# Attention and MLP in one kernel: another opening, DMA transposes for the later chunks, and the MLP's features loaded before attention

## The chip, the cores and the metric

The kernel runs on one core of a Trainium2 chip. The metric is the device time of one execution in microseconds (us); the span in a profile is a little shorter than the time of the execution it comes from. Engines: PE (TensorE, matrix products; PEld are its weight loads), DVE (VectorE), ACT (ScalarE), POOL (GpSimd) and SP (SyncE, which here only issues transfers). A "warm" matmul computes nothing that is used; it keeps PE busy.

## The reference

Shapes: x is 2048 x 640, 32 heads of 20, MLP width 1536.

```python
x  = A_x
xn = layernorm(x)                                   # no weights
qkv = (xn @ wqkv).reshape(B, S, 3, H, Dh)
p   = softmax(q @ k.T * Dh**-0.5)                   # per head
a   = (p @ v).reshape(B, S, D) @ wo
y   = layernorm(xn)
m   = gelu(y @ w1 + b1) @ w2 + b2                   # tanh form of gelu
out = x + a + m
```

## The kernel before, in words

Products run on f16 pairs: an f32 value is kept as a high half and a low half, and a product is three passes (`PASS`: high-high, high-low, low-high), accumulated in PSUM.

**Head** (lines 155 to 509, instruction order written out by hand). The 2048 rows are four chunks of 512 (`c`), each of four 128-row tiles (`j`). For a chunk, `norm_a` takes mean and variance on DVE and a power on POOL, `norm_b` refines it and normalises the four tiles in place, `norm_c` finishes the second norm's factor and writes it to `rscr`. `transp` turns the tiles on PE into PSUM tiles `pt`, two of the five 128-column slices (`k`) at a time; `transp_out` splits them into the halves `xnt` (ACT writes the high half, DVE the low one) and the last call writes the whole chunk to `xscr` for the MLP.

`qk(c, tt)` is one product of 30 matmuls for two of the ten 128-row blocks of Q and K, `qk_out` scales and splits it (`qkhl`), squares it (`sq`) and writes it to `qkscr`. `lengths` multiplies pending squares by `heads`, which gives squared lengths of every head's vectors; `shifts` makes one row `brow` of softmax shifts out of their maxima. `vproj(c, j)` is the V product of one tile, `vproj_out` puts it into `vfull`. The next chunk's norms and transposes are placed among the five `tt` steps of the current one. `some(n)` advances the preparation of w1 and w2 (squares for a scale, then splits) by n steps. `sums` and `scale_of` find a weight's power-of-two scale (the latter with a PE product `mxp`), `split_qkv` splits a weight of wqkv.

All of `transp`, `qk` and `vproj` share three PSUM tiles (`psS`, two banks each); `psO` and `psM` have one tile each.

**Attention** (lines 512 on). For each of 16 head pairs and two halves of the queries, groups of four 128-key blocks: `scores` on PE, exp on ACT, `rest` (a low half of some blocks) on DVE, and `pv` one group later. After the second block of each group a generator `fill` (the MLP, then the output projection) issues PE work: `credit` grows by `rate` = 1.235 a group, each step's cost is taken from it, and a stretch ends when credit or `CHUNK` is used up or an accumulation is complete. The MLP's first yield, 2.0, is a debt that the credit starts with. `load_chunk(mc)` loads 256 columns of features (`xm`) and their factors (`r2f`). `finish` divides by the softmax sums after a number of filler steps (`W1`, `W2` for the last) and writes `oscr`; `projection` loads a piece of it (`ot`) and the sum so far (`acc`), multiplies by wo (`z`) and writes the output.

Of the kernel before, what the change touches and what calls it, by code (L numbers as in the profile page):

```python
# [7 lines left out]
F32 = mybir.dt.float32  # L8
# [34 lines left out]
def mha_mlp_kernel(tc, x, wqkv, wo, w1, b1, w2, b2, out):  # L43
# [4 lines left out]
    with (  # L48
# [3 lines left out]
        tc.tile_pool(name="st", bufs=2) as stp,  # L52
        tc.tile_pool(name="psS", bufs=3, space=PSUM) as psS,
# [99 lines left out]


        with tc.tile_pool(name="pa", bufs=2) as pa, tc.tile_pool(name="pa1", bufs=1) as pa1, tc.manual_schedule():
# [46 lines left out]
            brow = pa1.tile([H, S], F16, name="brow")  # L202
# [33 lines left out]
            def norm_b(c):  # L236
# [5 lines left out]
                for j in range(4):  # L242
                    nc.vector.tensor_scalar(xts[c][j], xts[c][j], mv[:, j, 0:1], r[:, j : j + 1],
                                            ALU.subtract, ALU.mult)
                nc.vector.tensor_mul(ve, ve, mv[:, :, 1])
# [28 lines left out]

            PASS = ((0, 0), (0, 1), (1, 0))

            def qk(c, tt):
                ps = psS.tile([P, 2, 512], F32, tag="s", name="qkp")
                order = [(i, k) for i in range(2) for k in range(KD)]
                if c + tt == 0:  # L280

                    order = [(i, k) for k in range(KD) for i in range(2)]
                for i, k in order:
                    q, mm = divmod(2 * tt + i, KD)
                    for n, (a, b) in enumerate(PASS):
                        nc.tensor.matmul(ps[:, i, :], wv[:, k, q, a, mm * P : (mm + 1) * P],  # L286
                                         xnts[c][:, k, b, :], start=(k + n == 0), stop=(k == KD - 1 and n == 2))
                return ps
# [4 lines left out]
            def qk_out(c, tt, ps):  # L293
# [3 lines left out]
                sq = pa.tile([P, 2, 512], BF16, tag="sq", name="sq", bufs=2)  # L297
                for i0, i1 in parts:
# [3 lines left out]
                                                   ALU.mult, ALU.subtract)  # L302
                if c == 0:
# [3 lines left out]
                for s in range(2):  # L307
                    nc.sync.dma_start(
                        qkscr[s, 2 * tt * P : (2 * tt + 2) * P, c * 512 : (c + 1) * 512]
                        .rearrange("(i p) t -> p i t", p=P), hl[:, s])  # L310
                pend.extend((c, 2 * tt + i, sq[:, i]) for i in range(2))

            def lengths():

                for c, m, sq in pend:
# [10 lines left out]
                pend.clear()  # L326

            def shifts():
# [12 lines left out]
                nc.sync.dma_start(bscr[:H, :], brow)  # L341
# [37 lines left out]
            def split_qkv(n):  # L379
                q = "qkv".index(n)  # L380
                for k in range(KD):
                    nc.scalar.activation(wv[:, k, q, 0], stage[n][:, k], AF.Copy, scale=scales[n])
                    nc.vector.scalar_tensor_tensor(wv[:, k, q, 1], stage[n][:, k], scales[n], wv[:, k, q, 0],
                                                   ALU.mult, ALU.subtract)
# [61 lines left out]
            nc.gpsimd.memset(brow, KROW)  # L446
# [636 lines left out]
```

## Time and profile before

| | |
|---|---|
| median of 3 runs | 1384.71 us (1384.6 to 1388.05) |
| the profiled execution, its own time | 1385.2 us |
| its span | 1383.5 us |
| mean granted PE clock | 0.997 |
| busy PE / DVE / ACT | 1350.8 / 1061.7 / 1126.2 us |
| first Q/K product of the first chunk starts | 21.16 us |
| first scores start | 232.47 us |

A line of the timeline gives start, duration, engine, line of the code, operation, output and inputs, shapes and count; in brackets stands the idle time of the engine before it and what ended it. SPq is SP's queue, where the duration is that of the issuing, waits included. In a table of stages, PEclk is the granted clock as a share of full speed and DMA the busy share of the 16 DMA engines.

### The profile page before, as it was taken

The page shows a single profiled execution, that of the slowest core. Times are in us where ns is not written, and L with a number is a line of the kernel's source. Part 1 is how long each engine was busy: PE and PEld are TensorE (multiplying, and loading weights), DVE is VectorE, ACT ScalarE, POOL GpSimd, SP SyncE. Part 2 cuts the span into 40 slices and gives each one's busy share as a digit, 9 for nine tenths or more (in the row PEclk, how much of TensorE's full clock was granted, in tenths as well). Part 3 has the DMA queues.
Part 4 walks back from the last instruction along what each step waited for, and adds up shares of the span by engine and source line. Part 5 has one row for each costly group of instructions (what it writes and reads, how often), then busy time and mean ns, then how long its engine had stood idle before and what let it go on. Part 6 is the DMA issues. An engine that isn't in the chain of part 4 may idle for free.

```text
span 1383.5 us, 29113 instructions
## 1 busy us (share of the span) xinstructions
PE 1350.8 (98%) x11711; PEld 600.9 (43%) x11711; DVE 1061.7 (77%) x1425; ACT 1126.2 (81%) x1282; POOL 32.9 (2%) x75
## 2 busy tenths in 40 slices
PE   9999999999999999999999999999999999999998
PEld 6555555443333343433343333343334334333375
DVE  6648743899778977889887789877988897888642
ACT  5644323999999999999999999999999999999700
POOL 2000000000000000000000000000000000000000
PEclk9999999999999999999999999999999999999999
DMA  9853413012124231213221123212124322341375
GB/s 265 243 175 109 108 52 110 16 32 64 41 55 111 67 88 34 69 52 102 71 77 33 47 75 103 76 47 58 44 64 113 98 56 70 85 153 59 98 235 179
DMA packets 92320, 125.68 MB, mean 91 GB/s; under 512 B 16905, under 2 KB 58569, under 8 KB 92178
## 3 DMA queue, kind: packets, MB, share of 16 engines
q1 hardware_dynamic: 89218, 117.14, 28.3%
q0 software_dynamic: 2304, 5.24, 2.3%
q8 instruction: 94, 1.54, 0.5%
q10 hardware_dynamic: 656, 1.36, 0.3%
q14 instruction: 48, 0.39, 0.1%
HBM read 80.84 MB, written 42.86 MB: 89 GB/s over the span
## 4 chain that ended last, share of the span: by engine, by line
PE 59%; DVE 11%; ACT 5%; DMA 3%; issue 2%; SPq 1%; DVEq 0%; ACTq 0%
PE o L615 23%; PE s L584 14%; PE py L819 9%; PE pu L787 8%; DVE low L598 5%; PE z L896 5%; ACT p L586 4%; DMA oscr<-oa 1%; DVE u L740 1%; DMA oa<-opart 1%; DVE u L741 1%; DVE w L744 1%; DVE w L745 1%; DVE hT L752 1%; DVE u L750 1%
## 5 line engine op out<-in xcount | busy, mean ns | idle before, releaser
L586 ACT ACTIVATE p<-s 128x1024 f32<-128x1024 f32 x1024 | 973.6, 1042 | 52.4 <-PE s L584 46.2
L598 DVE TENSOR_TENSOR low<-p 128x1024 f16<-128x1024 f32 x512 | 608.8, 1219 | 165.0 <-ACT p L586 164.9
L615 PE MATMUL o<-p,vfull 128*32 128x512 bf16 (+1 forms) x4096 | 433.7, 494 | 0.0
L584 PE MATMUL s<-qs,ks 61*128 61x512 f16 x2048 | 317.7, 382 | 8.7 <-ACT p L586 7.2
L584 PEld LDWEIGHTS <-ks 61*128 61x128 f16 x2048 | 63.9, 94 | 296.4 <-issue 294.2
L787 PE MATMUL pu<-xm,w1t 128*128 128x256 f16 x1440 | 179.2, 274 | 4.1 <-DVE u L740 3.6
L819 PE MATMUL py<-w2t,hT 128*128 128x320 f16 x1152 | 178.6, 301 | 1.7 <-DVE xb L757 1.7
L787 PEld LDWEIGHTS <-w1t 128*128 128x128 f16 x1440 | 130.9, 98 | 71.2 <-issue 57.6
L819 PEld LDWEIGHTS <-hT 128*128 128x128 f16 x1152 | 102.5, 98 | 89.5 <-issue 55.2
L286 PE MATMUL qkp<-xnt,wv 128*128 128x512 f16 x600 | 132.3, 380 | 0.0
L615 PEld LDWEIGHTS <-vfull 128*32 128x32 f16 x3072 | 61.5, 95 | 146.2 <-issue 115.4
L615 PE MATMUL o<-low,vfull 128*32 128x512 f16 x1024 | 107.3, 379 | 6.6 <-DVE low L598 6.4
L300 ACT ACTIVATE qkhl<-qkp,qks 128x1024 f16<-128x1024 f32 (+1 forms) x24 | 23.3, 971 | 84.1 <-PE qkp L286 66.2
L286 PEld LDWEIGHTS <-wv 128*128 128x128 f16 x600 | 58.2, 98 | 67.8
L615 PEld LDWEIGHTS o<-p,vfull 128*32 128x32 f32 x2048 | 63.1, 109 | 50.6 <-issue 0.5
L349 PE MATMUL vp<-wv,xnt 128*128 128x320 f16 x480 | 66.6, 300 | 0.0
L896 PE MATMUL z<-w1t,ot 128*128 128x320 f16 x480 | 65.8, 300 | 0.0
L896 PEld LDWEIGHTS <-ot 128*128 128x128 f16 x480 | 46.7, 98 | 19.8 <-issue 1.7
L349 PEld LDWEIGHTS <-xnt 128*128 128x128 f16 x480 | 46.5, 98 | 18.2
L301 DVE SCALAR_TENSOR_TENSOR qkhl<-qkp,qks,qkhl 128x1024 f16<-128x1024 f32 (+1 forms) x24 | 26.5, 1104 | 34.3 <-ACT qkhl L300 34.3
L857 DVE SCALAR_TENSOR_TENSOR acc<-z,sc,acc 128x320 f32<-128x320 f32 x32 | 17.6, 550 | 45.1 <-PE z L896 42.9
L636 ACT ACTIVATE ev<-o 128x512 f32<-128x512 f32 x64 | 39.4, 615 | 3.3 <-PE o L615 3.3
(168 smaller groups left out, 685.7 us busy)
## 6 DMA issues: line engine op xcount, KB each, us to landing
qkscr<-qkhl SPq DMA_DIRECT2D x40, 256.0 KB
opart<-ev SPq DMA_DIRECT2D x124, 80.0 KB
ks<-qkscr SPq DMA_DIRECT2D x120, 80.0 KB
qs<-qkscr SPq DMA_DIRECT2D x192, 40.0 KB
oa<-opart SPq DMA_DIRECT2D x32, 240.0 KB
xt<-in_A_x_dram SPq DMA_DIRECT2D x16, 320.0 KB
xscr<-xnt SPq DMA_DIRECT2D x4, 1280.0 KB
xm<-xscr SPq DMA_DIRECT2D x8, 640.0 KB
```

Of the source, the lines that this page charges most:

```text
L286: nc.tensor.matmul(ps[:, i, :], wv[:, k, q, a, mm * P : (mm + 1) * P], xnts[c][:, k, b, :], start=(k + n == 0), stop=(k == KD - 1 and n == 2))
L300: nc.scalar.activation(hl[:, 0, i0:i1], ps[:, i0:i1], AF.Copy, scale=a)
L301: nc.vector.scalar_tensor_tensor(hl[:, 1, i0:i1], ps[:, i0:i1], a, hl[:, 0, i0:i1], ALU.mult, ALU.subtract)
L349: nc.tensor.matmul(ps[:, hf, :320], xnts[c][:, k, a, j * P : (j + 1) * P], wv[:, k, 2, b, hf * 320 : (hf + 1) * 320], start=(n == 0), stop ...
L584: nc.tensor.matmul(ps[:, a, :], ks[64 * a : 64 * a + 61, kb * P : (kb + 1) * P], qs[64 * a : 64 * a + 61, cc * 512 : (cc + 1) * 512], star ...
L586: nc.scalar.activation(pt, ps, AF.Exp, scale=QS)
L598: nc.vector.tensor_sub(low, pt, upper(pt))
L615: nc.tensor.matmul(pv.o[32 * q : 32 * q + 32, :], src[:, v0 - PAD * (1 - q % 2) :][:, :32], t, start=q not in pv.begun, stop=last, skip_gr ...
L636: nc.scalar.activation(evs[g, hf][:, cc], pv.o, AF.Copy)
L787: nc.tensor.matmul(ps[:, i], w1v[:, k, (f + i) // 4, a, fo_ : fo_ + P], xnt[:, k, b, :], start=(n == 0), stop=(n == 3 * KD - 1))
L819: nc.tensor.matmul(ps[:, :320], hTs[mc][:, f, a, j * P : (j + 1) * P], w2v[:, f, b, hf * 320 : (hf + 1) * 320], start=(n == 0), stop=(n == ...
L896: nc.tensor.matmul(ps[:, :320], ot[:, k, a, j * P : (j + 1) * P], wov[:, k, b, h * 320 : (h + 1) * 320], start=(n == 0), stop=(n == 3 * KD ...
```

## The change

- x's rows are loaded into two tiles of the pool `m2` (two 128-row tiles in each), which later hold the MLP's features, instead of five tiles of their own. `load_features` loads features; the first two calls stand in the head, at the third step of the last chunk.
- Opening: `brow` is a quarter as long and filled earlier; the first chunk is turned tile by tile into five separate banks, and then slice after slice is split together with the first 256 columns of that slice of wq. Columns 256 to 511 follow after the first product, the last 128 in the second step. Ten instead of twelve calls' worth of warm-up products. `norm_b2`, the second half of `norm_b`, is deferred for the first chunk, and `scale_of("k")` stands in the middle of the second product.
- The second chunk is turned on PE as before, but between the V products of the first. The third and fourth are turned by `turn`: ACT and DVE make the halves of a tile untransposed (`row`), and a transposing transfer on SP's queue writes them into `xnt`.
- `lengths` is called twice a chunk: for four blocks at the fourth step, and for six after the second V product (after the first in the last chunk). Squares of odd steps use another pool's tiles.
- Attention: the credit starts at 0 instead of -2, and in the first group, which has no `pv` yet, the filler gets a second turn.

```diff
+        tc.tile_pool(name="m2", bufs=2) as m2,
...
+        def load_features(mc):
+            xnt = m2.tile([P, KD, 2, MC], F16, tag="xnt", name="xm")
+            nc.sync.dma_start(xnt, xscr[:, :, :, mc * MC : (mc + 1) * MC])
+            return xnt
...
             def load_x(c):
                 xts[c] = []
                 for j in range(4):
-                    xt = pa.tile([P, D], F32, tag="xt", name="xt", bufs=5)
+                    if j % 2 == 0:
+                        pair = m2.tile([P, KD, 2, MC], F16, tag="xnt", name="xt").bitcast(F32)
+                        pair = pair.rearrange("p k s t -> p (k s t)")
+                    xt = pair[:, j % 2 * D : (j % 2 + 1) * D]
                     nc.sync.dma_start(xt, x2[c * 512 + j * P : c * 512 + (j + 1) * P, :])
...
-            brow = pa1.tile([H, S], F16, name="brow")
+            brow = pa1.tile([H, S // 4], F16, name="brow")
+            nc.gpsimd.memset(brow, KROW)
...
+                if c > 0:
+                    norm_b2(c)
+            def norm_b2(c):
+                mv, ve, r, r2 = rs[c]
                 nc.vector.tensor_mul(ve, ve, mv[:, :, 1])
                 nc.vector.tensor_scalar(ve, ve, EPS, None, ALU.add)
                 nc.gpsimd.tensor_tensor(r2, ve, nhalf, ALU.pow)
...
+            def turn(c, j):
+                if j == 0:
+                    xnts[c] = pa.tile([P, KD, 2, 512], F16, tag="xnt", name=f"xnt{c}")
+                xv = xts[c][j].rearrange("p (k n) -> p k n", k=KD)
+                row = pa.tile([P, KD, 2, P], F16, tag="row", name="row", bufs=3)
+                nc.scalar.activation(row[:, :, 0, :], xv, AF.Copy)
+                nc.vector.tensor_sub(row[:, :, 1, :], xv, row[:, :, 0, :])
+                nc.sync.dma_start(xnts[c].rearrange("p k s t -> p (k s) t")[:, :, j * P : (j + 1) * P],
+                                  row.rearrange("p k s n -> p (k s n)"), transpose=True)
+                if j == 3:
+                    nc.sync.dma_start(xscr[:, :, :, c * 512 : (c + 1) * 512], xnts[c])
+                    del xts[c]
...
-            def qk(c, tt):
+            def qk(c, tt, mid=None):
...
-                if c + tt == 0:
+                if c == 0 and tt < 2:
                     order = [(i, k) for k in range(KD) for i in range(2)]
...
+                    if mid and (i, k) == (1, 2):
+                        mid()
...
-            def lengths():
-                for c, m, sq in pend:
+            def lengths(n):
+                for c, m, sq in pend[:n]:
...
-                nc.sync.dma_start(bscr[:H, :], brow)
+                nc.sync.dma_start(bscr[:H, :].rearrange("h (r t) -> h r t", r=4), brow[:, None, :].to_broadcast([H, 4, S // 4]))
...
-            pts = []
-            transp(0, 0, pts)
-            scale_of("q")
-            transp(0, 2, pts)
-            transp(0, 4, pts)
-            warm(12)
-            for t in pts:
-                transp_out(*t)
-            split_qkv("q")
+            xnts[0] = pa.tile([P, KD, 2, 512], F16, tag="xnt", name="xnt0")
+            pts = [psS.tile([P, 2, 512], F32, tag="s", name="pt") for _ in range(2)]
+            pt = [pts[0][:, 0], pts[0][:, 1], pts[1][:, 0], pts[1][:, 1]]
+            for j in range(4):
+                if j == 3:
+                    scale_of("q")
+                    pt.append(psM.tile([P, 512], F32, tag="m", name="pt4"))
+                for k in range(KD - 1):
+                    nc.tensor.transpose(pt[k][:, j * P : (j + 1) * P], xts[0][j][:, k * P : (k + 1) * P], ident)
+            for j in range(4):
+                nc.tensor.transpose(pt[4][:, j * P : (j + 1) * P], xts[0][j][:, 4 * P :], ident)
+            warm(10)
+            for k in range(KD):
+                nc.scalar.activation(xnts[0][:, k, 0, :], pt[k], AF.Copy)
+                nc.vector.tensor_sub(xnts[0][:, k, 1, :], pt[k], xnts[0][:, k, 0, :])
+                split_qkv("q", [k], 0, 2 * P)
...
                 for tt in range(5):
-                    ps = qk(c, tt)
-                    lengths()
+                    if c == 0 and tt == 1:
+                        norm_b2(0)
+                        norm_c(0)
+                        ps = qk(0, 1, lambda: scale_of("k"))
+                        hl = qk_out(0, 0, first)
+                        split_qkv("q", c0=4 * P)
+                        split_qkv("k")
+                    else:
+                        ps = qk(c, tt)
+                    if tt == 3:
+                        lengths(4)
                     if c == 0:
                         if tt == 0:
+                            split_qkv("q", c0=2 * P, c1=4 * P)
                             sums("k", [stage["k"][:, 0:3], stage["k"][:, 3:]])
-                            norm_c(0)
-                            scale_of("k")
+                            first = ps
+                            continue
                         elif tt == 1:
-                            split_qkv("k")
-                            norm_a(1)
+                            qk_sq(0, 0, hl)
...
                     else:
-                        if nxt and tt < 3:
-                            (norm_a, norm_b, norm_c)[tt](nxt)
+                        step = tt - (c == 1)
+                        if nxt and 0 <= step < 3:
+                            (norm_a, norm_b, norm_c)[step](nxt)
                             some(1)
                         else:
                             some(2)
                     qk_out(c, tt, ps)
-                    if nxt and tt >= 2:
-                        pts = []
-                        transp(nxt, 2 * (tt - 2), pts)
-                        transp_out(*pts[0])
-                if c + 2 < 4:
-                    load_x(c + 2)
+                    if nxt and c > 0 and tt >= 2:
+                        for j in ((0,), (1, 2), (3,))[tt - 2]:
+                            turn(nxt, j)
+                    if c == 3 and tt == 2:
+                        early = [load_features(mc) for mc in range(2)]
+                if c == 1:
+                    load_x(3)
...
                 for j in range(4):
                     ps = vproj(c, j)
-                    lengths()
+                    if c == 0:
+                        if j == 0:
+                            norm_c(1)
+                        if j < 3:
+                            pts = []
+                            transp(1, 2 * j, pts)
+                            transp_out(*pts[0])
+                    if j == (0 if c == 3 else 1):
+                        lengths(10)
...
                     vproj_out(c, j, ps)
+                if c == 0:
+                    load_x(2)
...
             def mlp():
                 load_chunk(0)
                 load_chunk(1)
-                yield 2.0
+                yield 0.0
...
                             rest(units[0])
                             credit += rate
-                            spent, over[0] = 0.0, False
...
+                            other()
                         else:
                             for u in units[1:]:
                                 rest(u)
                             if prev:
                                 pv(prev)
+                            else:
+                                credit += rate
+                                other()
```

`other()` holds the loop that spends the credit, word for word as it stood. Not shown above: in the first chunk the second chunk's norms and v's scale and split come one step later.

More of the change, by code (lines that the diff above doesn't have):

```diff
@@ L770, in load_chunk @@
                 t0 = mc * MC
-                xnt = m2.tile([P, KD, 2, MC], F16, tag="xnt", name="xm")
-                r2f = m2.tile([P, MC], F32, tag="r2f", name="r2f")
-                nc.sync.dma_start(xnt, xscr[:, :, :, t0 : t0 + MC])
+                xnt = early.pop(0) if early else load_features(mc)
+                r2f = m1.tile([P, MC], F32, tag="r2f", name="r2f", bufs=2)
                 nc.sync.dma_start(r2f, rscr[None, t0 : t0 + MC].to_broadcast([P, MC]))
```

63 lines of the change are left out of this document (37 added, 26 removed).

## The prediction

> **What bounds the kernel now.** I read the page's busy shares and the chain that ended last first, then the timeline stage by stage, with the granted clock beside it.
>
> ```profile
> PE 1350.8 (98%) x11711; PEld 600.9 (43%) x11711; DVE 1061.7 (77%) x1425; ACT 1126.2 (81%) x1282; POOL 32.9 (2%) x75
> PE 59%; DVE 11%; ACT 5%; DMA 3%; issue 2%; SPq 1%; DVEq 0%; ACTq 0%
> 21.16 6.64 PE L286 MATMUL qkp<-xnt,wv 128*128 128x512 f16 x30
> 75.74 13.11 PE L286 MATMUL qkp<-xnt,wv 128*128 128x512 f16 x60
> 88.78 0.30 PE L321 MATMUL norms<-sq,heads 128*32 128x128 bf16 x8
> 89.01 6.65 PE L286 MATMUL qkp<-xnt,wv 128*128 128x512 f16 x30
> 220.14 12.40 PE L349 MATMUL vp<-wv,xnt 128*128 128x320 f16 x90
> 232.47 0.61 PE L584 MATMUL s<-qs,ks 61*128 61x512 f16 x4
> ```
>
> TensorE (PE) is the bound nearly everywhere: 98% busy, and the chain runs through it. So a change is worth what it takes off PE's own queue, or out of the few places where PE waits. The head (opening and projections) ends at 232.47, where the first scores start; attention with the MLP as filler follows, and then a tail of output projections.
>
> Prices on PE from these rows: one Q/K product of 30 matmuls is (88.78-75.74)/2 = 6.52 us; one V product is (232.47-220.14)/3 = 4.11 us; eight length matmuls take 89.01-88.78 = 0.23 us. The projection of a 512-row chunk is thus at least 5x6.52 + 4x4.11 = 49.0 us.
>
> **The opening.** Here PE waits and then runs at half clock.
>
> ```profile
> 1.07 11.38 PE L209 MATMUL warm<-ones 128*128 128x128 f32 x80 [1.07 <-POOL ones L174]
> 10.38 1.79 POOL L446 MEMSET brow<- 32x2048 f16 x1
> 10.85 1.36 DVE L217 TENSOR_SCALAR at<-at 128x4 f32<-128x4 f32 x1
> 24.24 0.17 DVE L217 TENSOR_SCALAR bt<-bt 128x4 f32<-128x4 f32 x1
> 12.83 2.18 DVE L243 TENSOR_SCALAR xt<-xt,mv,r 128x640 f32<-128x640 f32 x4
> 15.49 2.41 PE L262 MATMUL pt<-ident,xt 128*128 128x128 f32 x12
> 17.69 3.63 PE L209 MATMUL warm<-ones 128*128 128x128 f32 x24
> 8.00:10.00 2.00, 2.00 (x20) 1.00 1.02 402
> 16.00:17.00 1.00, 1.00 (x7) 0.50 0.11 29
> 50.75 1.09 PE L262 MATMUL pt<-ident,xt 128*128 128x128 f32 x8
> 51.68 6.64 PE L286 MATMUL qkp<-xnt,wv 128*128 128x512 f16 x30
> ```
>
> The two windows rows give PE's busy time with its instructions, the granted clock, the DMA share and GB/s. One tiny DVE step, L217, takes 1.36 us in the opening and 0.17 in the same code at 24.24; it ends at 12.21, just as the POOL memset of `brow` ends (12.17). The change issues that memset before the statistics and makes it a quarter as long, so L217 falls back to 0.17 and the four normalised rows of x come at 12.2, 12.7, 13.3 and 13.8 instead of from 13.4 to 15.0. The warm-up matmuls end at 12.45, so PE meets the first row at once: its gap there goes, and I take the clock to stay full. At full clock a transpose costs (51.68-50.75)/8 = 0.116 us, against 0.2 in the twelve at 15.49.
>
> Transposing row by row, PE does 20 transposes and the scale's matmul from 12.45 to about 15.1, the last slice's four among them. Then come 20 warm-up matmuls (ten calls instead of twelve) at 2.00/20 = 0.1 us: 17.1. Is the first slice there?
>
> ```profile
> 16.61 0.15 DVE L374 TENSOR_SCALAR s_q<-hi_q 128x1 f32<-128x1 f32 x1
> 48.17 3.69 ACT L382 ACTIVATE wv<-w1t,s_v 128x640 f16<-128x640 f32 x5
> 51.69 4.07 DVE L383 SCALAR_TENSOR_TENSOR wv<-w1t,s_v,wv 128x640 f16<-128x640 f32 x5
> 62.44 0.58 ACT L269 ACTIVATE xnt<-pt 128x512 f16<-128x512 f32 x1
> 63.05 0.69 DVE L270 TENSOR_TENSOR xnt<-pt,xnt 128x512 f16<-128x512 f32 x1 [0.29 <-ACT xnt L269]
> ```
>
> Before, s_q is there at 16.76, 1.75 us after the last normalised row; it now comes near 15.5. One slice is then 0.58 + some 0.4 us on ACT (256 of 640 columns of 0.74) and 0.69 + some 0.45 us on DVE, so slice 0 is complete near 16.6 and each further one 1.1 us later; PE takes six matmuls, 1.3 us, for a slice. The first product starts at 17.1 instead of 21.16: **4.0 us gained**. If the clock still halves, transposes at 0.2 and warm-ups at 3.63/24 = 0.15 put it at 19.9: 1.3. Nothing slower has a cause, so the bounds are 1 and 4.1.
>
> **The first chunk's stage.** It now lasts 75.74-21.16 = 54.6 us.
>
> ```profile
> 42.15 1.91 PE L262 MATMUL pt<-ident,xt 128*128 128x128 f32 x8 [0.39 <-DVE xt L243]
> 62.92 1.26 ACT L415 ACTIVATE junk<-w2t 128x1280 bf16<-128x1280 f32 x1
> 65.57 0.69 ACT L359 ACTIVATE vfull<-vp 128x640 f16<-128x640 f32 x1
> ```
>
> The eight transposes at 42.15 wait for norm_b(1) on DVE and hold PE 1.9 us, 1.0 more than the 0.93 at 50.75. In the new order all of chunk 1's transposes stand behind V products. PE's own work is 49.0 + 40 length matmuls 1.15 + 20 transposes 2.3 + three scale matmuls, priced like eight length matmuls, 0.7 = 53.2 us. But V products and transposes now alternate over three PSUM tiles, and between two of them ACT has up to 1.1 us of transp_out, two squares of 1.26 with their reads, some 2.7, and 0.7 of vproj_out, and DVE 0.8 behind it: a V tile is free some 5.3 us after the transposes, while PE comes back for one after 4.11 us and the lengths, 4.8. That is half a microsecond and more lost in each of two or three places. Also scale_of("k"), moved into the middle of the second product, makes DVE wait in order with qk_out(0, 0) and the splits of q's last columns and of k queued behind it, for which PE's third product then waits. I take 3 us of such waits (bounds 0 and 6): 56.2 us, **1.7 us lost**. norm_b2, norm_c and the deferred squares only change place on DVE and ACT inside this; rscr waits later on SP, and no transfer behind it is due.
>
> **The second and third chunks' stages.**
>
> ```profile
> 116.92 0.30 PE L321 MATMUL norms<-sq,heads 128*32 128x128 bf16 x8 [0.49 <-DVE sq L306]
> L125 ACT ACTIVATE wtmp<-w2t,s 128x640 f32<-128x640 f32 x12 | 9.8, 823 | 4.3 <-DVE w2t L127 4.2
> L127 DVE TENSOR_TENSOR w2t<-wtmp,w2t 128x640 f16<-128x640 f32 x12 | 9.9, 826 | 0.4
> 93.50:94.00 0.50, 0.50 (x4) 0.21 (x3) 0.00 (x0) 0.00 (x0) 0.00 (x0) 1.00 0.51 4
> rscr<-r SPq DMA_DIRECT2D x4, 2.0 KB
> 1255.47 1.66 DMA rb<-linv
> ```
>
> Twenty transposes, 2.3 us, leave PE in each; the 0.49 us wait for a square at 116.92 goes too, as the lengths come one V product later. So **2.8 and 2.3 us gained**. The lengths' matmuls stay as many, so calling them twice a chunk is worth nothing I can price. turn costs ACT and DVE 4x0.82 us a chunk each, about what transp_out cost; PE covers it.
>
> In their place stand four transposing transfers a chunk, which the trace does not show. One moves 128 x 1280 f16, 320 KB. Small pieces have a row: one rscr write is 512 pieces of 4 bytes (2.0 KB), and the window holding most of one (busy of PE, PEld, DVE, ACT and POOL, then clock, DMA share and GB/s) shows 0.51 x 0.5 us x 16 engines = 4.1 us, 8 ns a piece. In 32-byte pieces (10240) a turn is then 5.1 us; in 256-byte rows (1280) 0.64; by single elements (163840) 82. I take about 5, nearest to the middle. The cover: turn(2, 0) can go near 96.5 and chunk 2 starts near 124, so up to 27.5/4 = 6.9 us a turn costs nothing. The xscr write waits on SP for the last turn, with only the next load of x behind it. There can be no gain below zero, the PE side being counted already.
>
> The Trainium skill, "VectorE: DVE Perf Modes", "The three transpose paths", speaks against this: 1309 ns for one 128x128 block by the DMA crossbar, 390 ns on TensorE. Ten blocks singly would be an estimated 13.1 us a turn, and the sum would end near +40 us instead of -10. "DMA: Bandwidth & Descriptors", "Latency and other measured facts", gives 261 GB/s for such transfers, an estimated 1.3 us a turn, which leaves the sum as it is. No run here shows either.
>
> **The start of attention and the tail.**
>
> ```profile
> 239.00:240.00 1.00, 1.00 (x16) 0.50 1.14 329
> 241.55 0.61 PE L584 MATMUL s<-qs,ks 61*128 61x512 f16 x4
> 242.09 1.48 PE L787 MATMUL pu<-xm,w1t 128*128 128x256 f16 x12
> 291.16 1.65 PE o L615 x16
> 1339.27 0.96 SPq L851 DMA_DIRECT2D ot<-oscr  x2
> SPq L851 <- DMA oscr<-oa: 2.3, 1, 2.3
> 1324.37 45.75 PE z L896 x336
> ```
>
> From 232.47 to 241.55 PE does eight score pairs, six MLP matmuls and one group of P.V: 9.1 us, first in gaps behind exp, then at half clock (the windows row, columns as before). With the features loaded early and the credit starting at zero, some 30 MLP matmuls fill the gaps; eight pairs at 0.61/2, 30 matmuls at 1.48/12 and the P.V's 1.65 make 7.8: **1.3 us gained**, and 3.2 us of filler is done earlier. That comes off the tail as eight steps of three z matmuls at 45.75/336 = 0.136, 3.3 us. But the last ot load chain is paced by steps and by DMA: SP waited 2.3 us for oscr and issued at 1339.27, and the fifth piece's z starts, counted 144 matmuls after 1324.37, at 1344.0. With 24 matmuls fewer ahead PE is there at 1340.7, while ot lands (0.96 of issue and 1.7 or more, by the rb transfer) at 1342 or later. So 1.9 of the 3.3 go into a new wait: **1.4 us gained** (bounds 0 and 3.3).
>
> **Sum.** 4.0 - 1.7 + 2.8 + 2.3 + 1.3 + 1.4 = 10.1 us. The profiled execution took 1385.2 us around its span of 1383.5 and would become 1375.1; the median of the runs, 1384.71, is 0.5 below it and becomes 1374.6.
>
> **Rivals.** *Smaller gain:* the clock halves in the opening after all (2.7 less) and the first chunk's waits reach 6 us (3 less): 1380.3. For it, ACT is the fullest engine there; against it, PE's idle gap at 12.45 has a visible cause that goes.
>
> *Slower, by the transfers:* each turn's ten 128x128 blocks go one behind another, each at least the shortest landing here (rb<-linv, 1.66 us): 16.6 us a turn, four 66 us from 96.5, so chunk 2 starts at 163 instead of 124. 39 us twice, less 10.1: 1452. It decides against the change from (27.5+5.05)/4 = 8.1 us a turn. Against it, the bytes and the 8 ns pieces; for it, nothing here but an unseen kind of transfer. By the Trainium skill's 1309 ns a block (the section above) it would be an estimated 1424.
>
> *The filler's early start does nothing:* the tail's chain eats all of it and the start stays at exp's pace: 7.4 us gained, 1377.3. This lies inside my range.
>
> **How the numbers follow.** Forecast with its near variants 0.65; smaller gain 0.13; two of these losses together with stalls elsewhere, within 0.3% (4.2 us, about what a measurement of this kernel can tell from none) 0.08; slower by the transfers 0.14. So faster 0.78, same 0.08, slower 0.14. The low end takes no waits in the first stage and none in the tail (3 + 1.9 more): 1369.5; the high end takes the smaller gain, with a tail and a start worth a little less: 1383. What is left out is the slower case and a few hundredths beside it.
>
> **What would show it.** In the profile after: L217 at 0.17 in the opening; granted clock 1.0 from 12 to 20 and the first qkp matmul near 17; the first scores near 225.1; no pt matmuls after chunk 1's; no PE wait for a transfer at chunks 2 and 3; clock 1.0 through the start of attention; a short PE wait for ot in the tail. I am wrong if the first qkp matmul of chunk 2 waits for a DMA, if the opening's clock still falls to 0.5, or if the first chunk's stage grows by more than 5 us.

## The result, and the profile after

| | kernel before | changed kernel |
|---|---|---|
| time, median (lowest to highest) of 22 runs each | 1385.67 us (1383.9 to 1388.05) | 1382.66 us (1376.62 to 1385.66) |
| profiled execution, time and span | 1385.2 / 1383.5 us | 1382.63 / 1380.9 us |
| first Q/K product starts | 21.16 | 17.07 |
| stage of the first, second, third, fourth chunk | 54.6, 53.6, 52.7, 50.4 | 60.4, 50.0, 49.7, 49.8 |
| first scores, and the scores behind the first P.V | 232.47, 241.55 | 226.94, 234.36 |
| loop's end (`ev` of the last unit) | 1309.68 | 1302.12 |
| last step on VectorE (`acc`) | 1376.79 | 1374.03 |

The change is faster, by 0.25%: the ratio of the times is 0.9975 [0.9966, 0.9984]. The forecast was 10.1 us; 3.0 came. At the loop's end the changed kernel is 7.6 us ahead; at the last step it is 2.8 ahead.

The page of the changed kernel, its busy line and the engines' shares of the chain that ended last:

```profile
PE 1343.7 (97%) x11667; PEld 595.6 (43%) x11667; DVE 1061.3 (77%) x1439; ACT 1128.8 (82%) x1296; POOL 31.2 (2%) x75
PE 75%; DVE 12%; DMA 5%; ACT 5%; issue 2%; SPq 1%; POOL 0%; ACTq 0%; DVEq 0%
```

TensorE is busy 7 us less, and DMA has grown from 3% of the chain to 5%. The timeline of the changed kernel by TensorE, VectorE and GpSimd, up to the first scores (start, duration, instructions; in brackets the idle time before and what ended it):

```profile
7.23 0.51 POOL L213 MEMSET brow<- 32x512 f16 x1
10.69 0.17 DVE L228 TENSOR_SCALAR at<-at 128x4 f32<-128x4 f32 x1
12.25 1.61 PE L496 MATMUL pt<-ident,xt 128*128 128x128 f32 x12 [0.38 <-DVE xt L254]
17.07 10.52 PE L316 MATMUL qkp<-xnt,wv 128*128 128x512 f16 x48
57.15 1.92 PE L278 MATMUL pt<-ident,xt 128*128 128x128 f32 x8 [2.66 <-DVE xt L254]
60.12 7.05 PE L389 MATMUL vp<-wv,xnt 128*128 128x320 f16 x30 [1.06 <-DVE qkhl L332]
68.43 4.25 PE L389 MATMUL vp<-wv,xnt 128*128 128x320 f16 x30
77.47 26.06 PE L316 MATMUL qkp<-xnt,wv 128*128 128x512 f16 x120
127.50 26.06 PE L316 MATMUL qkp<-xnt,wv 128*128 128x512 f16 x120
226.94 0.61 PE L655 MATMUL s<-qs,ks 61*128 61x512 f16 x4
```

The opening is as forecast (17.07 against 17.1). The second and third chunks start without a wait for a transfer. The first chunk's stage has a 2.66 us gap at 54.5, a second of 1.06, and a V product that takes 7.05 us where the next takes 4.25. In the windows of those products (length, busy time of PE, PEld, DVE, ACT and POOL, then granted clock, DMA share, GB/s) the clock is down:

```profile
59.00:60.00 1.00, 0.07 (x1) 0.00 (x0) 1.00 (x2) 0.90 (x1) 0.93 (x1) 0.54 1.02 387
60.00:65.00 5.00, 4.88 (x19) 2.81 (x19) 2.59 (x7) 3.33 (x6) 0.00 (x0) 0.50 1.01 419
65.00:67.00 2.00, 2.00 (x13) 1.29 (x12) 0.00 (x0) 0.00 (x0) 0.00 (x0) 0.78 0.98 347
```

What comes before that gap, on ScalarE and VectorE:

```profile
52.86 1.11 ACT L331 ACTIVATE qkhl<-qkp,qks 128x1024 f16<-128x1024 f32 x1 [4.06 <-DMA qkscr<-qkhl]
54.01 1.28 DVE L332 SCALAR_TENSOR_TENSOR qkhl<-qkp,qks,qkhl 128x1024 f16<-128x1024 f32 x1 [3.99 <-ACT qkhl L331]
56.39 2.18 DVE L254 TENSOR_SCALAR xt<-xt,mv,r 128x640 f32<-128x640 f32 x4
58.78 1.28 DVE L332 SCALAR_TENSOR_TENSOR qkhl<-qkp,qks,qkhl 128x1024 f16<-128x1024 f32 x1
```

ScalarE waits 4.06 us for one of the two `qkhl` buffers, whose write to `qkscr` stands behind the load of w2 (issued at 35.41). VectorE waits with it in qk_out(0, 3), and behind that in VectorE's order stands norm_b(1), whose rows the transposes need.

The tail: the z and rb rows by TensorE, then the piece loads on SP, lt on ScalarE's queue and lt's first use on VectorE, all of the changed kernel:

```profile
1301.98 12.40 PE L966 MATMUL z<-w1t,ot 128*128 128x320 f16 x90
1316.81 2.97 PE L787 MATMUL rb<-lt,sel 64*80 64x64 f32 x32 [2.43 <-DVE lt L778]
1319.71 17.17 PE L966 MATMUL z<-w1t,ot 128*128 128x320 f16 x117
1339.32 0.72 PE L966 MATMUL z<-w1t,ot 128*128 128x320 f16 x2 [2.43 <-DMA ot<-oscr]
1306.88 1.19 SPq L921 DMA_DIRECT2D ot<-oscr  x2
1308.78 0.37 SPq L922 DMA_DIRECT2D acc<-accscr  x1
1308.80 1.15 ACTq L746 DMA_DIRECT2D lt<-lpart  x2
1315.39 0.22 DVE L773 TENSOR_TENSOR lt<-lt 64x64 f32<-64x64 f32 x1 [2.87 <-DMA lt<-lpart]
1317.00:1322.00 5.00, 5.00 (x41) 3.93 (x40) 0.03 (x1) 0.00 (x0) 0.00 (x0) 0.66 0.76 215
```

Where the kernel before ran from the loop's end through rb and z without a stop (rb at 1321.87, 2.50 us), TensorE now stops twice, for lt and for ot, 2.43 us each and 0.32 more for ot's second half; behind the first stop the clock is 0.66. The z matmuls cost 0.147 us each in the 117 behind rb, against 0.136.

### The profile page after: what moved, and what is told of

Read it like the earlier page. It is cut to its first block, busy times and chain, and to the rows that moved or that the text cites. A ratio compares the mean times of both kernels' runs of the same rounds, so it can differ in the third digit from the quotient of the medians.

```text
span 1380.9 us, 29065 instructions
## 1 busy us (share of the span) xinstructions
PE 1343.7 (97%) x11667; PEld 595.6 (43%) x11667; DVE 1061.3 (77%) x1439; ACT 1128.8 (82%) x1296; POOL 31.2 (2%) x75
## 4 chain that ended last, share of the span: by engine, by line
PE 75%; DVE 12%; DMA 5%; ACT 5%; issue 2%; SPq 1%; POOL 0%; ACTq 0%; DVEq 0%
PE o L686 24%; PE s L655 15%; PE py L889 10%; PE pu L857 9%; PE qkp L316 8%; PE vp L389 4%; DVE low L669 4%; ACT p L657 4%; PE z L966 4%; DMA oa<-opart 1%; DMA oscr<-oa 1%; DMA qkscr<-qkhl 1%; DVE u L811 1%; DVE u L812 1%; DVE w L815 1%
## 5 line engine op out<-in xcount | busy, mean ns | idle before, releaser
L686 PEld LDWEIGHTS <-vfull 128*32 128x32 f16 x3072 | 61.5, 95 | 146.2 <-issue 115.3
L966 PE MATMUL z<-w1t,ot 128*128 128x320 f16 x480 | 69.1, 306 | 2.8 <-DMA ot<-oscr 2.8
L389 PE MATMUL vp<-wv,xnt 128*128 128x320 f16 x480 | 69.7, 307 | 1.2 <-DVE qkhl L332 1.1
```

The lines of the kernel that those rows point to most:

```text
L389: nc.tensor.matmul(ps[:, hf, :320], xnts[c][:, k, a, j * P : (j + 1) * P], wv[:, k, 2, b, hf * 320 : (hf + 1) * 320], start=(n == 0), stop ...
L686: nc.tensor.matmul(pv.o[32 * q : 32 * q + 32, :], src[:, v0 - PAD * (1 - q % 2) :][:, :32], t, start=q not in pv.begun, stop=last, skip_gr ...
L966: nc.tensor.matmul(ps[:, :320], ot[:, k, a, j * P : (j + 1) * P], wov[:, k, b, h * 320 : (h + 1) * 320], start=(n == 0), stop=(n == 3 * KD ...
```

## Experiments

My theory had two parts: in the first chunk VectorE's order and then the clock, and in the tail a finish chain that no longer finds enough work beside it. The rivals: the PSUM and ScalarE waits that the prediction named; a cost of the transfers elsewhere; chance.

**e1_norm_early: VectorE's order in the first chunk.**

```
 (tt == 3)  split_qkv("v")
+           norm_b(1)
 (tt == 4)  nc.sync.dma_start(w1t, ...)
-           norm_b(1)
```

> The changed kernel with one edit: norm_b(1) stands right behind the splits of v's columns at tt == 3, ahead of qk_out(0, 3), instead of behind it. My theory: the first chunk's stage lost its time because qk_out(0, 3) sat on VectorE waiting for a transfer (qkhl's buffer, behind the load of w2) with norm_b(1) in the queue behind it, so the transposes of chunk 1 came late and TensorE idled until its clock fell. Then the normalise steps now end near 53.6 instead of 58.6, the transposes start near 55, vproj(0, 1) runs at clock 1.0 in 4.2 us instead of 7.05, the stage lasts some 55 us instead of 60.4, and the time falls by 5 to 6 us, to about 1377. The rival, the prediction's own reason (PSUM tiles and ScalarE's squares between V products): the order on VectorE matters little, the stage stays within 1 us of 60.4, and the time too.

Measured: 1377.22 us, ratio to before 0.9943 [0.9929, 0.9957]. The first stage lasts 71.80-16.87 = 54.9 us. ScalarE, VectorE and TensorE of this kernel:

```profile
52.69 1.11 ACT L331 ACTIVATE qkhl<-qkp,qks 128x1024 f16<-128x1024 f32 x1 [4.10 <-DMA qkscr<-qkhl]
50.92 2.18 DVE L254 TENSOR_SCALAR xt<-xt,mv,r 128x640 f32<-128x640 f32 x4
55.27 1.06 PE L278 MATMUL pt<-ident,xt 128*128 128x128 f32 x8 [0.92 <-DVE qkhl L332]
57.27 4.24 PE L389 MATMUL vp<-wv,xnt 128*128 128x320 f16 x30 [0.94 <-DVE qkhl L332]
```

ScalarE's wait is still there (4.10 us), but norm_b(1) is no longer behind it, and the clock stays up. So ScalarE's wait costs time only through the order on VectorE, and the rival falls. The length of the stage in one profile would not show it: e13 below, with norm_b(1) late, had 54.7 us, but there ScalarE waited only 1.15 us.

**e5_warm_gap: the clock by itself.**

```
+  if j == 0: warm(12, psM, "m")
   transp(1, 2 * j, pts)
+  if j == 0: warm(5, psM, "m")
```

> The changed kernel with warm-up matmuls put into TensorE's two gaps of the first chunk: twelve calls (24 instructions, 2.4 us) ahead of chunk 1's first transposes and five (1.0 us) behind them; nothing else moves. My theory: vproj(0, 1) takes 7.05 us because the idle 2.7 us and 1.1 us before it lower the clock to 0.5. With the gaps filled the clock stays 1.0 there, vproj(0, 1) takes 4.2 to 4.5 us, and the time falls by about 2.8 us, to about 1380; the wait for the normalised rows itself stays. The rival: those 30 matmuls are slow for another reason (PSUM or SBUF being read and written beside them), and neither their time nor the whole changes, or it grows by up to 1 us by the warm-ups.

Measured: 1378.93 us, 0.9956 [0.9942, 0.997]; the stage lasts 57.2 us.

```profile
59.72 4.24 PE L389 MATMUL vp<-wv,xnt 128*128 128x320 f16 x30
60.00:65.00 5.00, 5.00 (x56) 3.81 (x57) 2.26 (x4) 3.06 (x6) 0.00 (x0) 1.00 1.04 420
```

With the gaps filled the clock is 1.0 and the product takes 4.24 us: of the changed kernel's 60.4 us, 2.8 were slow matmuls and not waiting.

**e6_w2_act: the load in front of the writes.** `nc.sync.dma_start(w2t, ...)` became `nc.scalar.dma_start(w2t, ...)`.

> The changed kernel with the load of w2 (3.84 MB) issued from ScalarE's queue instead of SyncE's, at the same place in the program; nothing else moves. My theory: ScalarE waits 4.06 us for a qkhl buffer because the writes of qkhl stand behind that load in one queue. In a queue of their own they need not: ScalarE's wait falls under 1.5 us, norm_b(1) runs 2.5 us or more earlier, the wait for the normalised rows (2.66 us) falls under 1 us, and the time falls by 3 to 5 us. The rival: the engines of the transfers are full with w2's bytes whatever queue they come from, so the wait stays within 1 us of 4.06 and the time within 1 us.

Measured: 1377.38 us, 0.9936 [0.9919, 0.9952]; the stage lasts 54.2 us. ScalarE's qk_out(0, 3) no longer waits (2.25 us are left at qk_out(0, 4)) and the transposes start at 55.25 with no wait for the rows. So the place in the queue behind w2 mattered, not the bytes alone; the times say so more than the stage of one profile, their interval lying clear of the changed kernel's 0.9966 to 0.9984.

**e3_pe_turns: chunks 2 and 3 turned by TensorE again.** `turn(nxt, j)` became `transp(nxt, 2 * (tt - 2), pts); transp_out(*pts[0])`.

> The changed kernel with chunks 2 and 3 turned by TensorE behind qk_out (transp and transp_out) instead of by transfers: that part of the change undone. My theory: the transfers are hidden wholly, so undoing them costs TensorE's 2.3 us for the 20 transposes in each of two stages, and up to a microsecond of wait for PSUM each, as in the kernel before: 5 to 7 us more, about 1389. The rival: the transfers cost something elsewhere (VectorE and ScalarE for the rows, the queue to xscr), so that undoing them gives some of it back: 3 us more or less.

Measured: 1385.80 us, 0.9999 [0.9983, 1.0016], some 3.3 us more than the changed kernel; the two stages last 52.35 and 51.90 us instead of 50.03 and 49.68. That is the 20 transposes, 2.3 and 2.2 us, and nothing else: the expected extra waits for PSUM are missing, and the time expected, 1389, was too high. The transfers are hidden wholly.

**e2_rate and e4_start_old: the tail's share.** e2: `rate = 1.235` became 1.221. e4: `yield 0.0` is 2.0 again, and the first group's second `other()` is out.

> The changed kernel with one constant: rate 1.221 instead of 1.235, so that over the 256 groups 3.6 us less of filler is done inside the attention loop and some 27 z matmuls go back to the tail. My theory: the tail is now set by the last finish chain (lengths, reciprocal, rb, oscr, ot), which counts from the loop's end, and work done earlier only leaves TensorE with less to do beside it. Then the loop ends 3.6 us earlier, the waits before rb and before the fifth piece's z shrink from 2.4 and 2.7 us to under 1 each, the clock stays 1.0, and the time falls by 4 to 8 us, to about 1376. The rival: the loop isn't bound by TensorE alone, or the chain is late by its transfers whatever stands beside it: the tail grows by what the loop gives, and the time stays within 1.5 us.

> The changed kernel with the filler's start undone: the first yield is 2.0 again, and the first group has no second turn of the filler. My theory: at the changed kernel's rate the tail eats what the early start brings, and more: 3.2 us of filler go back to the tail. The start of attention grows by 1.3 to 1.7 us and the waits before rb and before ot shrink by 3 us and more with the clock drops behind them, so the time falls by 2 to 5 us, to about 1379. The rival, the prediction's step: the early start is a gain by itself, and undoing it costs 1.4 to 3 us.

Measured: e2 1372.42 us, 0.9904 [0.989, 0.9918]; e4 1376.74 us, 0.9936 [0.9923, 0.995]. Both waits go (ot keeps 0.8 and 0.4 us), the clock stays 1.0, and the gain is larger than I expected in both. Between the profiles of the changed kernel and e2 the loop is 5.2 us shorter, and the tail is 3.8 us shorter although 27 z matmuls (3.7 us) moved into it. TensorE of e2:

```profile
1295.00 0.99 PE L966 MATMUL z<-w1t,ot 128*128 128x320 f16 x6
1309.89 2.50 PE L787 MATMUL rb<-lt,sel 64*80 64x64 f32 x32
1333.12 25.98 PE L966 MATMUL z<-w1t,ot 128*128 128x320 f16 x190 [0.79 <-DMA ot<-oscr]
```

So undoing one part of the change, the filler's early start, makes the changed kernel faster by some 5.5 us. I had expected the start of attention to grow by 1.3 to 1.7 us in e4; it did not. TensorE of e4, from the first scores to those behind the first P.V:

```profile
226.09 0.61 PE L655 MATMUL s<-qs,ks 61*128 61x512 f16 x4
230.02 0.83 PE L857 MATMUL pu<-xm,w1t 128*128 128x256 f16 x6
233.49 0.60 PE L655 MATMUL s<-qs,ks 61*128 61x512 f16 x4
```

That is 7.40 us with 6 MLP matmuls; the changed kernel takes 7.42 with 30, the kernel before 9.08 with 6. The early filler runs in the gaps behind exp and neither shortens nor lengthens the start. The 1.7 us over the kernel before come without it: TensorE no longer waits 0.54 us for the features, and its clock stays 1.0 (0.50 in the kernel before). All that the early filler brings is work taken off the tail, and at this rate the tail is worse for it: 71.9 us with 447 z matmuls against e4's 67.7 with 474.

**e8_before_rate: the control.** Rate 1.221 in the kernel before.

> The kernel before with rate 1.221 instead of 1.235: a control for e2_rate. My theory: the kernel before has no wait in its tail, so the smaller rate has nothing to save there: 3.6 us of filler move from the loop to the tail, and the time stays within 2 us of before. The rival: 1.221 is better by itself (fewer stalls inside the loop), and the kernel before gains most of the 8 to 10 us that the changed one gained.

Measured: 1399.25 us, 1.0099 [1.0084, 1.0115]: slower by 13.7 us, which neither theory said. This kernel had more work left for the tail than any kernel so far, and yet:

```profile
1312.52 1.64 SPq L851 DMA_DIRECT2D ot<-oscr  x2
1324.42 4.49 PE L716 MATMUL rb<-lt,sel 64*80 64x64 f32 x32 [4.79 <-DVE lt L707]
ACT junk L541 <- DMA w1t<-in_A_wo_dram: 7.0, 1, 7.0
```

The last row is from the waits (total, times, longest): ScalarE, and with it exp, also stood 7.0 us for the load of wo, which is now issued at 1249.4, 0.1 us behind the first piece's ot and acc, instead of at 1232.3. "Too little work beside the chain" can't be the reason for a wait before rb here. The new theory: phase. The load of the next piece (ot and acc, 1280 KB) falls between the loop's end and lt, and lt comes late beside it.

**e9_both_121 and e12_rate_up: amount against phase.** e9: as e7 below, rate 1.21. e12: the changed kernel, rate 1.2525.

> As e7_both, but rate 1.21 instead of 1.221: another 2.8 us of filler go from the loop to the tail. My theory, sharpened by e8_before_rate: what hurts is where the load of the next piece (ot and acc, 1280 KB) falls. If it is issued between the loop's end and the transfer of lt, lt comes late and TensorE waits at rb; e2, e4 and e7 have that load some 2 us ahead of the loop's end. With 1.21 the first piece's z matmuls start only at the loop's end and the next load falls 2 to 4 us behind it: the wait before rb is back (2 to 5 us, with a clock drop behind it), and the time is 1371 to 1378, slower than e7. The rival: only the amount of work left beside the finish chain counts, so more of it is no worse: 1365 to 1368, no wait at rb.

> The changed kernel with rate 1.2525: 4.5 us more filler in the loop, so that the tail meets the pieces at the same phase as e2_rate (some 6 z of a piece done at the loop's end), but with a whole piece less to do. My theory of two separate causes: the wait before rb (a matter of phase) is under 0.7 us, and the wait for ot (a matter of the amount left beside the chain) grows from 2.8 us to 5 to 9 us. The time is then within 4 us of the changed kernel's. The rival, that both waits come from too little work: both grow, rb's above 2.4 us.

Measured: e9 1383.64 us, 0.9989 [0.9979, 0.9998]; e12 1384.42 us, 0.9994 [0.9983, 1.0006]. TensorE's waits in the tail, e9's row first, then e12's:

```profile
PE rb L787 <- DVE lt L778: 4.1, 1, 4.1
PE z L966 <- DMA ot<-oscr: 6.1, 2, 5.8
```

With more work left the wait before rb is back; with a whole piece less than e2, but the right phase, it is gone, and ot's wait has grown. Two causes, as expected. e9 is slower still than I expected, since ScalarE's wait for wo (6.6 us) is back too. The tails of all these kernels beside each other, with the issue of the next piece's ot counted from `ev`:

| kernel | ot issued, from the loop's end | lt waited for | TensorE waits at rb | TensorE waits for ot |
|---|---|---|---|---|
| before | -2.8 us | 0 | 0 | 0 |
| changed | +4.8 | 2.87 | 2.43 | 2.75 |
| e2, e4, e7 | -3.0, -2.8, -3.0 | 0 | 0 | 0.8, 0.4, 0.6 |
| e12 | -3.7 | 0 | 0 | 6.1 |
| e8, e9 | +3.8, +3.5 | 4.8, 4.5 | 4.8, 4.1 | 0 |

**e11_hold and e13_behind_lt: the load itself.** e11 held the load in the program until lt was asked for; e13 put it on lt's own queue:

```
-  nc.sync.dma_start(ot[...], ...)   # and acc
+  go = (nc.scalar if ended[0] and c < NMC // 2 else nc.sync).dma_start
+  go(ot[...], ...)
```

> The changed kernel (rate 1.235) with the load of a next piece held back, once the loop has ended, until the last finish has asked for lt: the load then stands behind lt instead of ahead of it; nothing else moves. My theory: lt lands 2.4 us or more earlier, the wait before rb and the clock drop behind it (1.7 us) go, and the time falls by 2 to 4 us, to about 1379.5, while the wait for ot (2.8 us) stays or grows, as the amount of work beside the finish chain is unchanged; the piece held back may itself be waited for, up to 1 us. The rival: lt is late because its own path (ev, lpart, lt) is long, not by the load: the wait at rb stays within 0.7 us of 2.4 and the time is the same or higher.

> The changed kernel (rate 1.235), with the piece loads that are issued after the loop's end and need nothing of the last finish (ot and acc of the third and fourth piece) put on ScalarE's queue, behind lt and oa, instead of SyncE's; nothing else moves. My theory, that this load ahead of lt makes lt late: the wait before rb falls from 2.4 us to under 0.7, the matmuls of rb run at full clock (2.5 us instead of 3.0), and the held piece's z may wait up to 1.5 us; the wait for ot stays at 2.8 us or more. In all 1.5 to 3.5 us less, about 1380. The rival, that lt's own path is long whatever goes beside it: the wait at rb stays above 1.7 us and the time within 1 us of the changed kernel's.

e11 was no experiment: the load stood behind lt in the program already, on another queue, so every engine's instruction order is the changed kernel's, and the load is still issued 4.8 us after the loop's end and lt 6.7. Its 1380.80 us, 0.9968 [0.9955, 0.998], only show the scatter. e13: 1382.41 us, 0.9982 [0.9968, 0.9996]. On ScalarE's queue and on TensorE:

```profile
1299.45 1.15 ACTq L746 DMA_DIRECT2D lt<-lpart  x2
1302.60 1.11 ACTq L922 DMA_DIRECT2D ot<-oscr  x2
1308.81 0.45 PE L967 MATMUL z<-w1t,ot 128*128 128x320 f16 x2 [1.38 <-DMA ot<-oscr]
1310.09 4.52 PE L787 MATMUL rb<-lt,sel 64*80 64x64 f32 x32
1334.70 0.72 PE L967 MATMUL z<-w1t,ot 128*128 128x320 f16 x2 [2.96 <-DMA ot<-oscr]
```

The wait before rb is gone, and the last step on lt (L778) ends 11.6 us after the loop's end instead of 14.6, so the load ahead of lt was its cause. The issue of lt itself comes 2.8 us earlier (3.9 instead of 6.7), so most of the delay arises before lt's own transfer starts. But the piece held back is waited for instead (1.38 and 0.59 us), the clock falls all the same (rb 4.52 us), ot is waited for 3.5 us once more, and the time does not move: my expectation of 1380 failed there. Repairing the order alone doesn't pay; the phase must be right.

**e10_memset and e14_memset_long: the opening.** e10 has brow's memset back behind the statistics, as four short ones; e14 adds one of the old length there.

> The changed kernel with the memset of brow put back behind the statistics, and done four times (four quarters, about 2 us of GpSimd as before the change): that part of the opening undone. My theory, from the prediction: the first small VectorE step beside it (0.17 us in the changed kernel) takes 1 us or more again, the normalised rows and the first Q/K product come about 1.2 us later (about 18.3 instead of 17.1), and if TensorE's gap is long enough the clock falls and it is nearer 19.5; the time rises by 1 to 2.5 us over the changed kernel's. The rival: the step was slow for another reason, it stays at 0.17 us and the first product at 17.1.

> The changed kernel with one more GpSimd memset behind the statistics, as long as brow's was before (32 x 2048 f16, into a part of the weights that is written later); nothing else moves. My theory: VectorE's small step beside a long memset takes 1.3 us instead of 0.17, the normalised rows come 1.2 us later, and the first Q/K product starts at 18.2 or later (19.9 if the clock falls too). The rival: the step's 1.36 us had another cause, it stays under 0.3 us and the first product within 0.3 us of 17.1.

Measured: e10 1381.14 us, 0.997 [0.9955, 0.9984]; e14, one run, 1380.32 us. VectorE's step and GpSimd's memset in e14:

```profile
9.71 1.79 POOL L486 MEMSET wv<- 32x2048 f16 x1
10.18 1.35 DVE L228 TENSOR_SCALAR at<-at 128x4 f32<-128x4 f32 x1
```

In e14 the step takes 1.35 us and ends as the memset does, as in the kernel before. In e10, beside memsets a quarter as long, it takes 0.17 us, and only the normalise steps are slower (2.62 against 2.18 us). The first product starts at 17.66 in e14 and at 17.54 in e10, against 17.07 in the changed kernel and 16.72 to 17.34 in the other kernels with its opening: the memset is worth some 0.5 us of the opening's 4.1, less than both expectations. The other 3.6 belong to the row-by-row transposes, the slices and the clock, which stays 1.0 in both; I did not take those apart.

How much that is depends on the profile of the kernel before. e8_before_rate has the same opening as that kernel, and these are its rows:

```profile
9.82 1.36 DVE L217 TENSOR_SCALAR at<-at 128x4 f32<-128x4 f32 x1
18.49 0.59 PE L286 MATMUL qkp<-xnt,wv 128*128 128x512 f16 x2
19.51 6.22 PE L286 MATMUL qkp<-xnt,wv 128*128 128x512 f16 x28 [0.43 <-DVE wv L383]
```

There the small step comes 1.0 us earlier, the clock stays 1.0, and the first product starts at 18.49, not at 21.16. Against that opening the changed kernel would gain 1.4 us at its first product.

**e7_both and e15_both_w2: the version that beats both.** e7 is e1 and e2 together; e15 adds e6.

> Both repairs together: norm_b(1) ahead of qk_out(0, 3), and rate 1.221. My theory: the two losses are separate (one in the head, one in the tail), so the gains add: from e2_rate's 1372.4 another 5 to 6 us go, about 1367, with the first chunk's stage near 55 us and at most 1 us of waits in the tail. The rival: a faster head only moves the phase of loop and tail again, and half or more of the 5.5 us comes back as a tail wait: 1370 or more.

> As e7_both (norm_b(1) earlier, rate 1.221), with the load of w2 on ScalarE's queue as in e6_w2_act. With norm_b(1) out of the way only 1.4 us of waits are left in the first chunk's V products (0.9 and 0.5 us), so by my theory this gives 0 to 1.4 us, 1366 to 1367.3. The rival: the load's place matters by itself (e6 had the shortest first stage, 54.2 us, with norm_b(1) late), and 2 us or more go: under 1365.

Measured: e7 1367.24 us (1367.0 to 1367.9), 0.9867 [0.9852, 0.9882]; e15 1367.27 us, 0.9863 [0.9841, 0.9885]. The gains add, and e15 adds nothing to them. e7 is 18.4 us faster than before by its ratio. Of the 17.3 us between the spans about 11.4 come up to the first scores, 1.7 in the start of attention and 5.5 in the loop (TensorE is busy 1.7 us less there and idle 3.8 us less); the tail takes 1.1 us more than before, with as many z matmuls (474).

## Why the prediction was right or wrong, step by step

- **Opening, 4.0 forecast: 4.1.** The step at L228 fell back to 0.17 us and the clock stayed 1.0, as said. That the memset mattered much there was too strong (0.5 us). That the size came out to 0.1 us is partly luck: it was forecast from, and measured against, a profile of the kernel before whose clock fell to 0.50; in e8 the same opening is 2.7 us shorter.
- **First chunk, -1.7 forecast: -5.8 in the profiled execution.** This step failed in its cause. I counted PSUM tiles and ScalarE's squares between V products and scale_of("k"). The runs showed norm_b(1), moved from tt == 2 to tt == 4 (two steps, where "The change" says one) and so behind qk_out(0, 3) on VectorE, which waits for a buffer whose write stands behind w2. My rule for a moved step, what stands ahead of it in its new place, was not applied to norm_b. And 2.8 us are the clock's answer to the gap. The size is not fixed: in nine profiles whose stage has the same code it was 54.7 to 61.5 us (middle 59.0), with ScalarE's wait between none (e10) and 4.68 us (e2); with norm_b(1) early it was 53.9 to 54.9 in four. That may be a part of why the changed kernel's runs lie 9 us apart and e7's within one; but e4's five runs, with norm_b(1) late, lie within 1.2 us, so this stays open.
- **Second and third chunks, +2.8 and +2.3: +3.6 and +3.0; fourth +0.7, not forecast.** Right for the transposes: e3 gives their part, 2.3 and 2.2. The lengths called twice a chunk, which I priced at nothing, are the likely rest: the fourth chunk has no transposes to lose and still gains 0.7. Its rows split that in two: 40 length matmuls take 0.79 us in two runs instead of 1.14 in five, and the five products, less often broken into, 32.5 us instead of 32.8. My price of 0.23 us for eight held for short runs only. That was not tried alone.
- **The transfers, my slower rival: refuted.** The third chunk's first product waits for nothing. SP's last turn of chunk 2 and the write behind it, which waits for that turn:

```profile
117.50 1.39 SPq L299 DMA_TRANSPOSE xnt<-row  x1
121.63 0.58 SPq L302 DMA_DIRECT2D xscr<-xnt  x1
```

A turn lands within 4.1 us of its issue; I took 5, and 8.1 was the point at which it hurts. The Trainium skill's price for a block by the DMA crossbar ("VectorE: DVE Perf Modes", "The three transpose paths"), an estimated 13.1 us for ten blocks one by one, does not hold for this form of transfer.
- **Start of attention, +1.3: +1.7.** The size was near (7.4 us with the clock at 1.0), the reason wrong in part: I counted the credit that starts at zero among the causes, and e4, without it, starts just as fast. What is left is the features loaded early and the clock; that was not tried alone.
- **Tail, +1.4: the time from the loop's end to the last step grew from 67.1 to 71.9 us with 27 z matmuls (3.7 us) fewer.** This step failed most: some 8.5 us of new loss where I priced one wait of 1.9. I followed the chain at its end, at ot, and there I was near (2.75 against 1.9), though my rows gave only 1.3 (ot at 1342, TensorE there at 1340.7) and I named no reason for the rest. I did not follow the piece loads, which filler done earlier moves against the loop's end. One fell ahead of lt: 2.43 us before rb. The clock behind both stops cost 2.7 more (rb 0.5, the next 117 z 1.25, the last 190 z 27.01 against e2's 25.98). The size is not fixed here either: in eight profiles with this rate and the tail's instruction order unchanged, the tail lasted 71.3 to 76.3 us, and the changed kernel's 71.9 is near the low end.

The sum with measured terms: 4.1 - 5.8 + 3.6 + 3.0 + 0.7 + 1.7 - 4.4 (loop and tail) = 2.9, against 2.6 between the spans. My "filler's early start does nothing" was the right rival with the wrong floor: at this rate it did harm, while e7, which keeps it, has no such loss.

## What to carry to other kernels

When a step is moved, list what stands ahead of it in its new place on its engine, and for each of those what it waits for: a normalise step of 2 us cost 5.5 because the instruction before it waited for a transfer. When filler is done earlier, redraw the end as well: the loads that the filler issues move against the chain that starts at the loop's end, and a constant (here the rate, 1.1% less) can be worth more than the change, and cost 13.7 us in the kernel before. A wait of TensorE of 1 us or more can bring slow matmuls behind it, and they belong in the price: here 2.75 us for waits of 5.2 (the changed kernel's tail), 3.3 for waits of 1.97 (e13, before rb), and nothing in e3's first chunk.

## What the runs showed of the hardware

- Idle time of TensorE of 1 to 3 us brought the granted clock down to 0.5 to 0.7 for some microseconds: in the changed kernel's first chunk (gaps of 2.66 and 1.06 us, clock 0.50) and before its rb (2.43 us, 0.66), in e1 before rb (2.2 us, 0.50), in e13 (1.38 and 0.59 us, 0.51) and in e11 (1.39 us, 0.56 from 2 us behind the gap on). But the length of the gaps does not decide it: in e3's first chunk TensorE was idle 3.0 us between 54 and 59 (gaps of 1.73 and 1.06) and the clock stayed 1.00, while in e10 it was idle 1.5 us in the same stretch (gaps of 0.25 and 1.06) and the clock fell to 0.50. What does decide it stays open. The Trainium skill ("TensorE: Matmul & The Clock Gate", Part 1) has the low clock after an idle window of about 3.4 us; here less idle time than that was enough.
- A one-input VectorE step of 4 elements a partition takes 1.35 us beside a 1.79 us memset of GpSimd and 0.17 beside memsets of a quarter of that length. The Trainium skill ("GPSIMD Engine Reference", "Key points") says that the two share their way into SBUF; that it matters how long the other's instruction is, is what these two runs add. In e14 the two-input step just ahead of it, beside the same memset, took its usual 0.17 us (at 9.98).
